# Reordering the head of a squared-ReLU MLP: x loads first, tail columns transposed in pairs, small loads moved between queues

## The chip, the cores and the metric

The kernel runs on one core of a Trainium2 chip. The metric is the device time of one execution in microseconds (us); lower is better. A profiled execution also gives a span, from the first to the last instruction, which is a little shorter than the device time.

## The reference

```python
# x (1, 2048, 576), w1 (576, 4608), b1 (4608), w2 (4608, 576), b2 (576), all bf16
h = jnp.einsum("bsd,df->bsf", x, w1) + b1
r = jnp.where(h > 0, h, 0)
h = r * r
out = jnp.einsum("bsf,fd->bsd", h, w2) + b2
```

It is a two-layer MLP whose hidden activation is the squared ReLU. The inner sizes are awkward in one place: D = 576 is four and a half times 128, so each contraction over D has four full chunks of 128 rows and a tail of 64.

## The kernel before, in words

The 2048 rows of x are worked in four blocks of 512 columns (`sb` 0 to 3). Phase A computes the hidden tile: for each of 36 groups of 128 hidden features it multiplies a piece of w1 with the transposed x block `xT` and writes `r = relu(h + b1)` on ACT (L176) and `hT = r * r` on DVE (L177). Phase B multiplies `hT` with w2 into the first 448 output columns (`phase_b`, L289), phase T does the last 128 output columns transposed (`phase_t`, L270, with the bias `b2T` added on ACT at L273).

Of the 36 feature groups, G = 4 are computed in `a_full` from full 128-row weights `w1n` plus the 64 tail rows `w1n8`; the other 32 are computed in `a_rows` as two halves of the array, 64 rows each, with weights `w_h` (`w1_h` in the code). For that the transposed block is kept in a nine-slot window buffer `xTw` with slots named E3 = 0, O = 1 to 4, SPC = 5, E = 6 to 8; slots 5 to 8 are copies, with upper and lower half partitions exchanged, that `dup_windows` writes on DVE (L119, L120).

Blocks 1 to 3 get their `xT` by DMA transposes on the SP queue (L126, L127). Block 0 can't wait for those. Its four row tiles of x are loaded plainly into `x_sb` (L72), transposed on PE against the identity matrix (`x_transpose`, L149), and copied out of PSUM by DVE and ACT (`x_copies`, L156 to L159). In the k_outer order, block 0's `a_full` weaves these transposes between groups of four matmuls of 256 columns (`part(h, k)`, L227), so that the first parts can run before all of x has been transposed. The tail chunk is taken as the 128 columns 448 to 575, a fifth transpose per row tile. After the parts come the four tail matmuls (`pair`, L203 and L205) and then `a_rows(0)`.

`keep` puts an instruction at its place in program order on its engine. Each engine then works its own list from top to bottom, and DMAs are issued from the lists of SP, ACT and POOL. Ahead of all this stand seven matmuls on constants (`WARM`, L63). POOL builds the identity, clears `b1_rows`, issues the load of b1 (L98) and of the last 128 values of b2 (`b2_col`, called b_col in the profile, L100), and then casts the latter into `b2T` (L102). All other loads are on SP, but for two x tiles on ACT. The SP list is: x 0, w1n 0, w1n 1, x 3, w1n 2, w1n 3, two `w_h` pieces, the two `w1n8` halves, twelve `w_h` pieces, the transposes of block 1, four `w_h` pieces, the broadcast of b2 (`b_bc`), four chunks of w2 (`w_sb`), the transposes of block 2.

Of the kernel before, what the change touches and what calls it, by code (L numbers as in the profile page):

```python
# [11 lines left out]
BF16 = mybir.dt.bfloat16  # L12
FP32 = mybir.dt.float32
# [4 lines left out]
def kernel(  # L18
# [9 lines left out]
    nc = tc.nc  # L28
    keep = tc.keep_in_program_order
    P = 128  # L30
    H = 64
    x2 = x.flatten_outer_dims()
    out2 = out.flatten_outer_dims()
    S, D = x2.shape
    F = w1.shape[1]
    NFT = F // P
    NC = D // H
    NK = NC // 2
    G = 4
    GW = G * P  # L40
# [4 lines left out]
    RT = SB // P  # L45
    DT = P
    DM = D - DT

    const = ctx.enter_context(tc.tile_pool(name="const", bufs=1))
    wpool = ctx.enter_context(tc.tile_pool(name="wpool", bufs=1))  # L50
# [5 lines left out]
    ps_h = ctx.enter_context(tc.tile_pool(name="ps_h", bufs=4, space=PSUM))  # L56
    ps_o = ctx.enter_context(tc.tile_pool(name="ps_o", bufs=4, space=PSUM))

    wps = ps_o.tile([P, 512], FP32, name="wps", tag="po")
    ones = nc.const_aps.tensor(1.0, [P, 512], BF16)  # L60
    WARM = [512] * 6 + [128]
    for i, n in enumerate(WARM):
        keep(nc.tensor.matmul(wps[:, 0:n], lhsT=ones[:, 0:P], rhs=ones[:, 0:n], start=True, stop=True))  # L63

    xs = const.tile([P, RT, D], BF16, name="x_sb")
    w1n = wpool.tile([P, NK, GW], BF16, name="w1n")
    w1n8 = wpool.tile([P, G // 2, P], BF16, name="w1n8")
    w1_h = wpool.tile([P, NC, FH], BF16, name="w1_h")
    w1_v = w1.rearrange("(c p) f -> p c f", p=H)

    def load_x(eng, rt):
        keep(eng.dma_start(out=xs[:, rt, :], in_=x2[rt * P:(rt + 1) * P, :]))  # L72

    def load_w1n(eng, k):
        keep(eng.dma_start(out=w1n[:, k, :], in_=w1[k * P:(k + 1) * P, 0:GW]))

    def load_w1n8(eng, h):
        src = w1[NK * P:D, 0:GW].rearrange("p (i h f) -> p i h f", h=2, f=P)
        keep(eng.dma_start(out=w1n8[h * H:(h + 1) * H, :, :], in_=src[:, :, h, :]))

    def load_w1(eng, h, j0, j1):
        keep(eng.dma_start(out=w1_h[h * H:(h + 1) * H, :, j0 * P:j1 * P],
                      in_=w1_v[:, :, GW + h * FH + j0 * P:GW + h * FH + j1 * P]))

    load_x(nc.sync, 0)
    load_x(nc.scalar, 1)
    load_w1n(nc.sync, 0)
    load_x(nc.scalar, 2)
    load_w1n(nc.sync, 1)
    load_x(nc.sync, 3)  # L90
    for k in range(2, NK):
        load_w1n(nc.sync, k)

    ident = const.tile([P, P], BF16, name="ident")
    make_identity(nc, ident[:])
    b1_rows = const.tile([P, P], BF16, name="b1_rows")
    nc.gpsimd.memset(b1_rows[:], 0.0)
    nc.gpsimd.dma_start(out=b1_rows[0:NFT, :], in_=b1.rearrange("(ft p) -> ft p", p=P))  # L98
    b2_col = const.tile([P, 1], BF16, name="b2_col")
    nc.gpsimd.dma_start(out=b2_col[:], in_=b2[DM:D].rearrange("(d o) -> d o", o=1))  # L100
    b2T = const.tile([P, 1], FP32, name="b2T")
    nc.gpsimd.tensor_copy(out=b2T[:], in_=b2_col[:])  # L102
    warm = const.tile([P, 1], FP32, name="warm")
    keep(nc.scalar.activation(out=warm[:], in_=nc.const_aps.tensor(0.0, [P, 1], FP32), func=ACT.Relu))

    E3, O, SPC, E = 0, 1, 5, 6
    LO_W = [O, O + 1, O + 2, O + 3, E, E + 1, E + 2, E3, SPC]
# [9 lines left out]
    def dup_windows(sb):  # L117
        xT = xT_blk[sb]
        keep(nc.vector.tensor_copy(out=xT[0:H, SPC:SPC + 4, :], in_=xT[H:P, E3:E3 + 4, :]))  # L119
        keep(nc.vector.tensor_copy(out=xT[H:P, SPC:SPC + 4, :], in_=xT[0:H, O:O + 4, :]))  # L120
# [7 lines left out]

    w2_sb = wpool.tile([P, NFT, D], BF16, name="w2_sb")
    w2_view = w2.rearrange("(ft p) d -> p ft d", p=P)  # L130
    W2CH = 9

    def load_w2(c):
        keep(nc.sync.dma_start(out=w2_sb[:, c * W2CH:(c + 1) * W2CH, :], in_=w2_view[:, c * W2CH:(c + 1) * W2CH, :]))
# [3 lines left out]
    alloc_xT(0)  # L138
    xT0 = xT_blk[0]
    HS = SB // 2  # L140
    tb_po = [ps_o.tile([P, 2, HS], BF16, name="tb", tag="po") for _ in range(2)]
    tb_ph = [ps_h.tile([P, 2, HS], BF16, name="tb", tag="ph") for _ in range(4)]
    half_banks = [tb_ph, None]

    def x_transpose(j, k):
        h, q = divmod(j, 2)
        qc = slice(q * P, (q + 1) * P)
        bank, slot, c0 = (half_banks[h][k], 0, k * P) if k < NK else (half_banks[h][2], 1, D - P)
        keep(nc.tensor.transpose(bank[:, slot, qc], xs[:, j, c0:c0 + P], ident[:]))  # L149

    def x_copies(h):
        hc = slice(h * HS, (h + 1) * HS)
        for k in range(NK):
            src = half_banks[h][k][:, 0, :]
            if k % 2 == 0:
                keep(nc.vector.tensor_copy(out=xT0[:, O + k, hc], in_=src))  # L156
            else:
                keep(nc.scalar.copy(out=xT0[:, O + k, hc], in_=src))
        keep(nc.vector.tensor_copy(out=xT0[:, E3, hc], in_=half_banks[h][2][:, 1, :]))  # L159


    b1T = const.tile([P, NFT], FP32, name="b1T")

    def make_b1T():
        b1T_ps = ps_o.tile([P, P], BF16, name="b1T_ps", tag="po")
        keep(nc.tensor.transpose(b1T_ps[:], b1_rows[:], ident[:]))  # L166
        keep(nc.vector.tensor_copy(out=b1T[:], in_=b1T_ps[:, 0:NFT]))

# [26 lines left out]
    def a_full(sb, order):  # L195
        xT = xT_blk[sb]
        banks = []
        for g in range(G):
            pool, tag = (ps_o, "po") if g < 2 else (ps_h, "ph")
            banks.append(pool.tile([P, SB], FP32, name="pn", tag=tag))  # L200

        def pair(i, start, stop):
            keep(nc.tensor.matmul(banks[2 * i][:], lhsT=w1n8[0:H, i, :], rhs=xT[0:H, SPC, :],  # L203
                             start=start, stop=stop, skip_group_check=order == "k_outer"))
            keep(nc.tensor.matmul(banks[2 * i + 1][:], lhsT=w1n8[H:P, i, :], rhs=xT[H:P, E3, :],  # L205
                             start=start, stop=stop, skip_group_check=order == "k_outer"))

        def full(g, k, start, stop):
            keep(nc.tensor.matmul(banks[g][:], lhsT=w1n[:, k, g * P:(g + 1) * P], rhs=xT[:, O + k, :],  # L209
                             start=start, stop=stop))  # L210

        if order == "rows_first":
            for i in (1, 0):
                pair(i, True, False)
            for g in (2, 3, 0, 1):
                for k in range(NK):
                    full(g, k, False, k == NK - 1)
                evac_h(sb, banks[g], g)
        else:
            if order == "k_outer":  # L220
                tb_new = [ps_h.tile([P, 2, HS], BF16, name="tb", tag="ph") for _ in range(2)]
                half_banks[1] = tb_new + tb_po

                def part(h, k):
                    hc = slice(h * HS, (h + 1) * HS)
                    for g in range(G):
                        keep(nc.tensor.matmul(banks[g][:, hc], lhsT=w1n[:, k, g * P:(g + 1) * P],  # L227
                                              rhs=xT[:, O + k, hc], start=(h == 0 and k == 0), stop=False,
                                              skip_group_check=True))

                for j in range(2):
                    for k in range(NK):
                        x_transpose(j, k)
                for j in range(2):
                    x_transpose(j, NK)
                x_copies(0)
                part(0, 0)
                for k in range(NK + 1):
                    x_transpose(2, k)
                part(0, 1)  # L240
                part(0, 2)
                for k in range(NK + 1):
                    x_transpose(3, k)
                x_copies(1)
                dup_windows(0)
                part(0, 3)
                part(1, 0)
                make_b1T()
                for k in range(1, NK):
                    part(1, k)  # L250
            else:
                for g in (2, 3, 0, 1):
                    for k in range(NK):
                        full(g, k, k == 0, False)
            for i in (1, 0):
                pair(i, False, True)
                evac_h(sb, banks[2 * i], 2 * i)
                evac_h(sb, banks[2 * i + 1], 2 * i + 1)
# [35 lines left out]
    for (j0, j1) in [(0, 1), (1, 2), (2, 4), (4, 6), (6, 8), (8, 10), (10, 12)]:  # L294
        load_w1(nc.sync, 0, j0, j1)
        load_w1(nc.sync, 1, j0, j1)
        if j0 == 0:
            load_w1n8(nc.sync, 0)
            load_w1n8(nc.sync, 1)
    load_xT(1)  # L300
    for (j0, j1) in [(12, 14), (14, 16)]:
        load_w1(nc.sync, 0, j0, j1)
        load_w1(nc.sync, 1, j0, j1)
    keep(nc.sync.dma_start(out=b2_bc[:], in_=b2.partition_broadcast(P)))
    for c in (0, 2, 1, 3):
        load_w2(c)
    load_xT(2)

# [51 lines left out]
```

## Time and profile before

| what | value |
|---|---|
| time, median of 3 runs | 290.72 us (290.65 to 291.53) |
| the profiled execution's own time | 291.46 us |
| its span | 289.6 us |
| granted TensorE clock | 1.000 |
| PE busy | 285.5 us, 99% of the span |
| ACT busy | 96.7 us, 33% |
| DVE busy | 78.6 us, 27% |
| POOL busy | 2.3 us, 1% |

The profiled execution took 1.86 us more than its span. PE is busy nearly all the time; its busy figure is an upper bound on useful work, since matmuls overlap and their ends are modelled. The other engines wait for PE. The columns of a timeline row are the start in us, the length in us, the engine, the line, the operation, its output and input, the number of instructions merged into the row, and in brackets the idle time before it with what ended it. In engine names, SPq and POOLq are the queues from which DMAs are issued; the length of such a row is the time of the issue, not of the transfer.

### The profile page before, as it was taken

Reading aid. Unit: us, or ns where it says so; the run is one execution under the profiler, and the core shown is the slowest. Engines: PE = TensorE matmul, PEld = TensorE weight load, DVE = VectorE, ACT = ScalarE, POOL = GpSimd, SP = SyncE. Lnnn points to the kernel's source line nnn. Section 1 sums busy time; section 2 is a strip of 40 time slices with the busy share of each in tenths; the row PEclk is TensorE's granted clock in tenths of the full one; section 3 lists DMA queues with packets and bytes.
Section 4 is the critical chain, followed back from the end, with each engine's and each line's share of the span. In section 5 each row is a group of like instructions: output and inputs, shape, how many; then the busy total and the mean of one; then the engine's idle time right before and its main releaser. Section 6 shows DMA issues by size and latency. Waiting matters only on the chain.

```text
span 289.6 us, 4693 instructions
## 1 busy us (share of the span) xinstructions
PE 285.5 (99%) x2027; PEld 139.9 (48%) x2032; DVE 78.6 (27%) x176; ACT 96.7 (33%) x154; POOL 2.3 (1%) x10
## 2 busy tenths in 40 slices
PE   8999999999999999999999999999999999999996
PEld 5544444444444555555544444444444455555555
DVE  1644554444500200000015444444440001100001
ACT  2566666666500000000027666666670000000000
POOL 3000000000000000000000000000000000000000
PEclk9999999999999999999999999999999999999999
DMA  7999999400001200000000000000000110000000
GB/s 198 221 245 188 308 389 212 92 0 2 0 14 25 52 16 18 16 16 18 16 16 2 1 2 0 2 0 2 0 2 0 36 38 16 16 16 19 33 16 18
DMA packets 31605, 16.52 MB, mean 57 GB/s; under 512 B 15700, under 2 KB 31584, under 8 KB 31584
## 3 DMA queue, kind: packets, MB, share of 16 engines
q1 hardware_dynamic: 31232, 15.91, 22.3%
q10 hardware_dynamic: 288, 0.30, 0.4%
q8 instruction: 16, 0.26, 0.4%
q14 instruction: 5, 0.04, 0.0%
q0 software_dynamic: 64, 0.01, 0.0%
HBM read 11.36 MB, written 2.36 MB: 47 GB/s over the span
## 4 chain that ended last, share of the span: by engine, by line
PE 98%; DMA 1%; issue 0%; DVE 0%
PE ph L188 42%; PE po L289 38%; PE pt L270 11%; PE pn L209 4%; PE pn L227 1%; DMA x_sb<-in_x_dram 1%; PE tb L149 1%; PE ph L190 1%; PE pn L203 1%; DVE o_sb L291 0%; PE b1T_ps L166 0%; PE pn L205 0%
## 5 line engine op out<-in xcount | busy, mean ns | idle before, releaser
L190 PE MATMUL ph<-xTw,w_h 64*128 64x512 bf16 x576 | 124.6, 376 | 0.0
L188 PE MATMUL ph<-xTw,w_h 64*128 64x512 bf16 x576 | 124.6, 376 | 0.0
L289 PE MATMUL po<-w_sb,hT 128*128 128x448 bf16 (+2 forms) x612 | 109.4, 341 | 0.0
L176 ACT ACTIVATE r<-ph,b1T 128x512 bf16<-128x512 f32 x128 | 81.1, 685 | 41.6 <-PE ph L190 41.6
L188 PEld LDWEIGHTS <-w_h 64*128 64x128 bf16 x576 | 54.1, 94 | 68.3
L289 PEld LDWEIGHTS <-hT 128*128 128x128 bf16 x612 | 58.5, 98 | 51.0
L177 DVE TENSOR_TENSOR hT<-r 128x512 bf16<-128x512 bf16 x144 | 61.2, 426 | 75.9 <-ACT r L176 75.5
L190 PEld LDWEIGHTS <-w_h 64*128 64x128 bf16 x576 | 54.1, 94 | 0.0
L291 DVE TENSOR_TENSOR o_sb<-po,b_bc 128x448 bf16<-128x448 f32 (+2 forms) x17 | 10.2, 597 | 125.8 <-PE po L289 125.8
L270 PE MATMUL pt<-hT,w_sb 128*128 128x512 bf16 x142 | 31.3, 379 | 0.1
L176 ACT ACTIVATE r<-pn,b1T 128x512 bf16<-128x512 f32 x16 | 10.3, 688 | 61.0 <-PE pn L205 59.6
L270 PEld LDWEIGHTS <-w_sb 128*128 128x128 bf16 x144 | 14.1, 98 | 17.0
L273 ACT ACTIVATE oT<-pt,b2T 128x512 bf16<-128x512 f32 x4 | 2.8, 688 | 28.3 <-PE pt L270 28.3
L209 PE MATMUL pn<-xTw,w1n 128*128 128x512 bf16 x45 | 10.4, 379 | 0.4 <-issue 0.3
L209 PEld LDWEIGHTS <-w1n 128*128 128x128 bf16 x48 | 4.5, 98 | 6.0 <-issue 0.8
L227 PE MATMUL pn<-xTw,w1n 128*128 128x256 bf16 x32 | 4.6, 295 | 0.0
L63 PE MATMUL wps<-const-bfloat16-1.0 128*128 128x512 bf16 (+1 forms) x7 | 2.8, 582 | 0.8 <-PEq L344 0.8
L227 PEld LDWEIGHTS <-w1n 128*128 128x128 bf16 x32 | 3.3, 107 | 0.5
L156 DVE COPY xTw<-tb 128x256 bf16<-128x256 bf16 x4 | 1.1, 292 | 6.7 <-PE tb L149 6.7
L119 DVE COPY xTw<-xTw 64x2048 bf16<-64x2048 bf16 x4 | 2.8, 690 | 0.2
L120 DVE COPY xTw<-xTw 64x2048 bf16<-64x2048 bf16 x4 | 2.7, 687 | 0.1
L149 PE MATMUL tb<-ident,x_sb 128*128 128x128 bf16 x20 | 2.4, 288 | 0.2 <-DMA x_sb<-in_x_dram 0.2
(23 smaller groups left out, 15.2 us busy)
## 6 DMA issues: line engine op xcount, KB each, us to landing
w_sb<-in_w_dram SPq DMA_DIRECT2D x4, 1296.0 KB, 12.7
w_h<-in_w_dram SPq DMA_DIRECT2D x14, 288.0 KB, 6.2
out_dram<-o_sb SPq DMA_DIRECT2D x15, 112.0 KB, 1.7
w_h<-in_w_dram SPq DMA_DIRECT2D x4, 144.0 KB, 3.5
w1n<-in_w_dram SPq DMA_DIRECT2D x4, 128.0 KB, 3.9
out_dram<-ot SPq DMA_DIRECT2D x4, 128.0 KB, 2.0
x_sb<-in_x_dram ACTq DMA_DIRECT2D x2, 144.0 KB, 2.9
x_sb<-in_x_dram SPq DMA_DIRECT2D x2, 144.0 KB, 3.4
```

What stands on the lines that cost most here:

```text
L63: keep(nc.tensor.matmul(wps[:, 0:n], lhsT=ones[:, 0:P], rhs=ones[:, 0:n], start=True, stop=True))
L149: keep(nc.tensor.transpose(bank[:, slot, qc], xs[:, j, c0:c0 + P], ident[:]))
L176: keep(nc.scalar.activation(out=r[:], in_=bank[:], func=ACT.Relu, bias=b1T[:, ft:ft + 1], scale=1.0))
L177: keep(nc.vector.tensor_tensor(out=hTs[sb][:, ft, :], in0=r[:], in1=r[:], op=ALU.mult))
L188: keep(nc.tensor.matmul(bx[:], lhsT=w1_h[0:H, LO_C[i], jc], rhs=xT[0:H, LO_W[i], :], start=(i == 0), stop=(i == NC - 1)))
L190: keep(nc.tensor.matmul(by[:], lhsT=w1_h[H:P, UP_C[i], jc], rhs=xT[H:P, UP_W[i], :], start=(i == 0), stop=(i == NC - 1)))
L203: keep(nc.tensor.matmul(banks[2 * i][:], lhsT=w1n8[0:H, i, :], rhs=xT[0:H, SPC, :], start=start, stop=stop, skip_group_check=order == "k_o ...
L209: keep(nc.tensor.matmul(banks[g][:], lhsT=w1n[:, k, g * P:(g + 1) * P], rhs=xT[:, O + k, :], start=start, stop=stop))
L227: keep(nc.tensor.matmul(banks[g][:, hc], lhsT=w1n[:, k, g * P:(g + 1) * P], rhs=xT[:, O + k, hc], start=(h == 0 and k == 0), stop=False, s ...
L270: keep(nc.tensor.matmul(pt[:], lhsT=w2_sb[:, ft, DM:D], rhs=hT[:, ft, :], start=(i == 0), stop=(i == NFT - 1)))
L289: keep(nc.tensor.matmul(po[:, 0:d1 - d0], lhsT=hT[:, ft, jj * P:(jj + 1) * P], rhs=w2_sb[:, ft, d0:d1], start=(i == 0), stop=(i == NFT - 1)))
L291: keep(nc.vector.tensor_tensor(out=o_sb[:, d0:d1], in0=po[:, 0:d1 - d0], in1=b2_bc[:, d0:d1], op=ALU.add))
```

## The change

The order of the first loads is now x 0 and x 2 on SP, x 1 and x 3 on ACT, then w1n 0 and 2 on SP and w1n 1 and 3 on ACT. The two `w1n8` loads move from SP to ACT and take the whole 512 columns for each half (1 KB a row, where they were two pieces of 256 bytes), and the load of b1 moves from POOL to ACT. `b1_rows` is cleared on DVE. The load of `b2_col` moves from POOL to SP, where it stands behind all `w_h` pieces; its cast into `b2T` stays on POOL. w2 comes in two chunks instead of four.

The transposes of block 0 are all done ahead of the parts. Each row tile has four transposes of full chunks. For the tail, POOL copies the 64 tail columns of two row tiles side by side into a new tile `xs8`, and one transpose then serves two row tiles: 16 + 2 transposes instead of 20. The new `x_copies_tail` takes them apart on DVE, with copies that also make the windows of block 0.

The PSUM banks are dealt differently (transposes and b1 in `ps_h`, the four `a_full` banks of block 0 in `ps_o`), and the seventh warm-up matmul has 256 columns instead of 128.

In the list that the built program gives each engine, POOL has after the identity these three instructions, in this order: the cast of `b2T`, which waits for the `b2_col` load, and the two copies into `xs8`. PE has the 16 full transposes, then the two tail transposes, each of which waits for its POOL copy, and then the first part. On SP, the load of `b2_col` stands behind two x tiles, two w1n chunks, fourteen `w_h` pieces, the two transposes of block 1 and four more `w_h` pieces.

```diff
-    wps = ps_o.tile([P, 512], FP32, name="wps", tag="po")
+    wps = ps_h.tile([P, 512], FP32, name="wps", tag="ph")
-    WARM = [512] * 6 + [128]
+    WARM = [512] * 6 + [256]
...
-    w1n8 = wpool.tile([P, G // 2, P], BF16, name="w1n8")
+    w1n8 = wpool.tile([P, GW], BF16, name="w1n8")
...
     def load_w1n8(eng, h):
-        src = w1[NK * P:D, 0:GW].rearrange("p (i h f) -> p i h f", h=2, f=P)
-        keep(eng.dma_start(out=w1n8[h * H:(h + 1) * H, :, :], in_=src[:, :, h, :]))
+        keep(eng.dma_start(out=w1n8[h * H:(h + 1) * H, :], in_=w1[NK * P:D, 0:GW]))
...
+    b1_rows = const.tile([P, P], BF16, name="b1_rows")
+    nc.vector.memset(b1_rows[:], 0.0)
     load_x(nc.sync, 0)
     load_x(nc.scalar, 1)
-    load_w1n(nc.sync, 0)
-    load_x(nc.scalar, 2)
-    load_w1n(nc.sync, 1)
-    load_x(nc.sync, 3)
-    for k in range(2, NK):
-        load_w1n(nc.sync, k)
+    load_x(nc.sync, 2)
+    load_x(nc.scalar, 3)
+    for k in range(NK):
+        load_w1n(nc.sync if k % 2 == 0 else nc.scalar, k, k + 1)
...
-    b1_rows = const.tile([P, P], BF16, name="b1_rows")
-    nc.gpsimd.memset(b1_rows[:], 0.0)
-    nc.gpsimd.dma_start(out=b1_rows[0:NFT, :], in_=b1.rearrange("(ft p) -> ft p", p=P))
-    b2_col = const.tile([P, 1], BF16, name="b2_col")
-    nc.gpsimd.dma_start(out=b2_col[:], in_=b2[DM:D].rearrange("(d o) -> d o", o=1))
-    b2T = const.tile([P, 1], FP32, name="b2T")
-    nc.gpsimd.tensor_copy(out=b2T[:], in_=b2_col[:])
     warm = const.tile([P, 1], FP32, name="warm")
     keep(nc.scalar.activation(out=warm[:], in_=nc.const_aps.tensor(0.0, [P, 1], FP32), func=ACT.Relu))
+    for h in range(2):
+        load_w1n8(nc.scalar, h)
+    keep(nc.scalar.dma_start(out=b1_rows[0:NFT, :], in_=b1.rearrange("(ft p) -> ft p", p=P)))
...
-    W2CH = 9
+    W2CH = 18
...
-    def x_transpose(j, k):
+    def x_transpose(j):
         h, q = divmod(j, 2)
-        qc = slice(q * P, (q + 1) * P)
-        bank, slot, c0 = (half_banks[h][k], 0, k * P) if k < NK else (half_banks[h][2], 1, D - P)
-        keep(nc.tensor.transpose(bank[:, slot, qc], xs[:, j, c0:c0 + P], ident[:]))
+        for k in range(NK):
+            bank, slot = PLACE[k]
+            keep(nc.tensor.transpose(tb[h][bank][:, slot, q * P:(q + 1) * P], xs[:, j, k * P:(k + 1) * P], ident[:]))
+
+    def x_transpose_tail(h):
+        keep(nc.gpsimd.tensor_copy(out=xs8[:, 2 * h:2 * h + 2, :], in_=xs[:, 2 * h:2 * h + 2, NK * P:D]))
+        keep(nc.tensor.transpose(tb[1][0][:, 2, h * P:(h + 1) * P], xs8[:, 2 * h:2 * h + 2, :], ident[:]))
+
+    def x_copies_tail():
+        src = tb[1][0][:, 2, :].rearrange("p (h t) -> p h t", h=2)
+        for q in range(2):
+            keep(nc.vector.tensor_copy(out=xT0_q[H:P, E3, :, q, :], in_=src[q * H:(q + 1) * H, :, :]))
+        for q in range(2):
+            keep(nc.vector.tensor_copy(out=xT0_q[0:H, SPC, :, q, :], in_=src[q * H:(q + 1) * H, :, :]))
+        keep(nc.vector.tensor_copy(out=xT0[0:H, E:E + 3, :], in_=xT0[H:P, O:O + 3, :]))
+        keep(nc.vector.tensor_copy(out=xT0[0:H, E3, :], in_=xT0[H:P, O + 3, :]))
+        keep(nc.vector.tensor_copy(out=xT0[H:P, SPC:SPC + 4, :], in_=xT0[0:H, O:O + 4, :]))
 
     def x_copies(h):
         hc = slice(h * HS, (h + 1) * HS)
-        for k in range(NK):
-            src = half_banks[h][k][:, 0, :]
-            if k % 2 == 0:
-                keep(nc.vector.tensor_copy(out=xT0[:, O + k, hc], in_=src))
-            else:
-                keep(nc.scalar.copy(out=xT0[:, O + k, hc], in_=src))
-        keep(nc.vector.tensor_copy(out=xT0[:, E3, hc], in_=half_banks[h][2][:, 1, :]))
+        for k in (0, 1):
+            keep(nc.vector.tensor_copy(out=xT0[:, O + k, hc], in_=tb[h][0][:, k, :]))
+        keep(nc.scalar.copy(out=xT0[:, O + 2:O + 4, hc], in_=tb[h][1][:, 0:2, :]))
...
                 for j in range(2):
-                    for k in range(NK):
-                        x_transpose(j, k)
-                for j in range(2):
-                    x_transpose(j, NK)
+                    x_transpose(j)
                 x_copies(0)
-                part(0, 0)
-                for k in range(NK + 1):
-                    x_transpose(2, k)
-                part(0, 1)
-                part(0, 2)
-                for k in range(NK + 1):
-                    x_transpose(3, k)
+                for j in range(2, RT):
+                    x_transpose(j)
                 x_copies(1)
-                dup_windows(0)
-                part(0, 3)
+                for h in range(2):
+                    x_transpose_tail(h)
+                x_copies_tail()
+                for k in range(NK):
+                    part(0, k)
                 part(1, 0)
                 make_b1T()
...
-        if j0 == 0:
-            load_w1n8(nc.sync, 0)
-            load_w1n8(nc.sync, 1)
     load_xT(1)
     for (j0, j1) in [(12, 14), (14, 16)]:
         load_w1(nc.sync, 0, j0, j1)
         load_w1(nc.sync, 1, j0, j1)
+    b2_col = const.tile([P, 1], BF16, name="b2_col")
+    keep(nc.sync.dma_start(out=b2_col[:], in_=b2[DM:D].rearrange("(d o) -> d o", o=1)))
+    b2T = const.tile([P, 1], FP32, name="b2T")
+    nc.gpsimd.tensor_copy(out=b2T[:], in_=b2_col[:])
     keep(nc.sync.dma_start(out=b2_bc[:], in_=b2.partition_broadcast(P)))
-    for c in (0, 2, 1, 3):
+    for c in range(2):
         load_w2(c)
```

More of the change, by code (lines that the diff above doesn't have):

```diff
@@ L72, in load_x, with load_w1n @@
         keep(eng.dma_start(out=xs[:, rt, :], in_=x2[rt * P:(rt + 1) * P, :]))
-    def load_w1n(eng, k):
-        keep(eng.dma_start(out=w1n[:, k, :], in_=w1[k * P:(k + 1) * P, 0:GW]))
+    def load_w1n(eng, k0, k1):
+        src = w1[k0 * P:k1 * P, 0:GW].rearrange("(k p) f -> p k f", p=P)
+        keep(eng.dma_start(out=w1n[:, k0:k1, :], in_=src))
     def load_w1n8(eng, h):
-        src = w1[NK * P:D, 0:GW].rearrange("p (i h f) -> p i h f", h=2, f=P)
-        keep(eng.dma_start(out=w1n8[h * H:(h + 1) * H, :, :], in_=src[:, :, h, :]))
+        keep(eng.dma_start(out=w1n8[h * H:(h + 1) * H, :], in_=w1[NK * P:D, 0:GW]))
     def load_w1(eng, h, j0, j1):
@@ L140 @@
     HS = SB // 2
-    tb_po = [ps_o.tile([P, 2, HS], BF16, name="tb", tag="po") for _ in range(2)]
-    tb_ph = [ps_h.tile([P, 2, HS], BF16, name="tb", tag="ph") for _ in range(4)]
-    half_banks = [tb_ph, None]
-    def x_transpose(j, k):
-        h, q = divmod(j, 2)
-        qc = slice(q * P, (q + 1) * P)
-        bank, slot, c0 = (half_banks[h][k], 0, k * P) if k < NK else (half_banks[h][2], 1, D - P)
-        keep(nc.tensor.transpose(bank[:, slot, qc], xs[:, j, c0:c0 + P], ident[:]))
+    tb = [[ps_h.tile([P, 4, HS], BF16, name="tb", tag="ph") for _ in range(2)] for _ in range(2)]
@@ new lines @@
+    PLACE = [(0, 0), (0, 1), (1, 0), (1, 1)]
+    xs8 = const.tile([P, RT, H], BF16, name="xs8")
+    xT0_q = xT0.rearrange("p c (h q t) -> p c h q t", h=2, q=2)
+    def x_transpose(j):
+        h, q = divmod(j, 2)
+        for k in range(NK):
[4 more added lines that the diff above has]
+        keep(nc.tensor.transpose(tb[1][0][:, 2, h * P:(h + 1) * P], xs8[:, 2 * h:2 * h + 2, :], ident[:]))
@@ L162 @@
+        keep(nc.scalar.copy(out=xT0[:, O + 2:O + 4, hc], in_=tb[h][1][:, 0:2, :]))
     b1T = const.tile([P, NFT], FP32, name="b1T")
     def make_b1T():
-        b1T_ps = ps_o.tile([P, P], BF16, name="b1T_ps", tag="po")
+        b1T_ps = ps_h.tile([P, P], BF16, name="b1T_ps", tag="ph")
         keep(nc.tensor.transpose(b1T_ps[:], b1_rows[:], ident[:]))
@@ L198, in a_full @@
         for g in range(G):
-            pool, tag = (ps_o, "po") if g < 2 else (ps_h, "ph")
+            pool, tag = (ps_o, "po") if g < 2 or order == "k_outer" else (ps_h, "ph")
             banks.append(pool.tile([P, SB], FP32, name="pn", tag=tag))
         def pair(i, start, stop):
-            keep(nc.tensor.matmul(banks[2 * i][:], lhsT=w1n8[0:H, i, :], rhs=xT[0:H, SPC, :],
+            keep(nc.tensor.matmul(banks[2 * i][:], lhsT=w1n8[0:H, 2 * i * P:(2 * i + 1) * P], rhs=xT[0:H, SPC, :],
                              start=start, stop=stop, skip_group_check=order == "k_outer"))
-            keep(nc.tensor.matmul(banks[2 * i + 1][:], lhsT=w1n8[H:P, i, :], rhs=xT[H:P, E3, :],
+            keep(nc.tensor.matmul(banks[2 * i + 1][:], lhsT=w1n8[H:P, (2 * i + 1) * P:(2 * i + 2) * P], rhs=xT[H:P, E3, :],
                              start=start, stop=stop, skip_group_check=order == "k_outer"))
@@ L220, in a_full @@
             if order == "k_outer":
-                tb_new = [ps_h.tile([P, 2, HS], BF16, name="tb", tag="ph") for _ in range(2)]
-                half_banks[1] = tb_new + tb_po
                 def part(h, k):
```

## The prediction

> **What bounds the kernel now.** I read the page's totals first, then the chain of waits in order of time for the head, then the timelines of POOL and SP, since the change moves work on those two.
>
> ```profile
> span 289.6 us, 4693 instructions
> PE 285.5 (99%) x2027; PEld 139.9 (48%) x2032; DVE 78.6 (27%) x176; ACT 96.7 (33%) x154; POOL 2.3 (1%) x10
> ```
>
> PE has no slack: whatever holds PE for a microsecond adds a microsecond. The change touches only the head, so the head is what I price. Its chain of waits (start, length, what):
>
> ```profile
> 0.73 2.99 DMA x_sb<-in_x_dram
> 3.73 0.04 issue
> 3.77 1.25 PE tb L149 x10
> 5.02 0.86 PE pn L227 x4
> 5.88 0.53 PE tb L149 x5
> 6.42 0.98 PE pn L227 x8
> 7.40 0.28 PE tb L149 x5
> 7.68 0.87 PE pn L227 x8
> 8.55 0.06 PE b1T_ps L166
> 8.61 1.31 PE pn L227 x12
> 9.92 0.32 PE pn L203
> ```
>
> From 3.77 us the chain stays on PE until the tail matmuls (L203; the timeline starts them at 9.85). There is no hole left to fill. The first four parts take 0.86/4 = 0.215 us each and eight later ones 0.87/8 = 0.109 us: PE runs at half rate until a little after 6 us, although PE has been at work since 0.78.
>
> Now POOL and SP, from the timelines of these engines (start, length, engine; brackets: idle before):
>
> ```profile
> 2.14 0.56 POOL L100 DMA_DIRECT2D b_col<-in_b_dram  x1
> 5.72 0.18 POOL L102 CAST b2T<-b_col 128x1 f32<-128x1 bf16 x1 [3.03 <-DMA b_col<-in_b_dram]
> ```
>
> ```profile
> 18.29 4.57 SPq L126 DMA_TRANSPOSE xTw<-in_x_dram  x1
> 22.91 1.25 SPq L127 DMA_TRANSPOSE xTw<-in_x_dram  x1
> 24.21 2.65 SPq L82 DMA_DIRECT2D w_h<-in_w_dram  x4
> 26.91 0.82 SPq L304 DMA_DIRECT2D b_bc<-in_b_dram  x1
> 27.77 10.21 SPq L134 DMA_DIRECT2D w_sb<-in_w_dram  x4
> ```
>
> The load of b_col is issued at 2.14, and its cast on POOL waits 3.03 us for it. Nothing stands behind that cast on POOL, so the wait is free. On SP, the slot just behind the last `w_h` piece, where the change puts this load, comes at 26.9 us. The DMA issues say when things from there land: for the window of the last `w_h` issue (26.2 us), and on the page,
>
> ```profile
> w_h<-in_w_dram SPq DMA_DIRECT2D x1, 288.0 KB, 6.6
> ```
>
> ```profile
> b_bc<-in_b_dram SPq DMA_DIRECT2D x1, 144.0 KB, 6.5
> ```
>
> so the last `w_h` lands at 26.2 + 6.6 = 32.8 and b_bc at 26.9 + 6.5 = 33.4 us.
>
> **What the Trainium skill says.** "Trainium Architecture — The Big Picture", section "Inside one NeuronCore": each engine has its own instruction stream and the engines meet only through semaphores. So what stands behind a waiting instruction on its engine waits too. The trace agrees for SP: its L275 waits 77.6 us for ACT, and SP issues nothing meanwhile. For POOL no case is shown. "DMA: Bandwidth & Descriptors", section "Queues, rings and completion order": descriptors of a ring are consumed in order, and the completion increment lands only after every earlier write from that DMA engine. The trace agrees: the issue-to-landing time of the 288 KB pieces grows from about 4 us (at 7 us) to 7.7 us (at 12 us) as the backlog grows, and b_bc lands 0.6 us after the piece ahead of it. "TensorE: Matmul & The Clock Gate", section "What's actually happening": an idle window of about 3.4 us puts PE back to half rate, and a busy one of about 3.4 us, with a free-running phase, restores it. The half-rate parts above agree with the start; no stall of that length is in the trace of before.
>
> **The change, part by part.**
>
> *The wait.* POOL's list is now: identity, cast of b2T, two copies into xs8. PE's list is: 16 transposes, two tail transposes on xs8, then all 32 parts. The cast waits for b2_col, the xs8 copies stand behind the cast, the tail transposes wait for the copies, and every part stands behind the tail transposes. So PE stops after 16 transposes, about 5.8 us, until b2_col lands. On PE, everything is behind it; ACT and DVE wait for PE.
>
> *When b2_col lands.* SP loses ahead of it two w1n issues (0.9 us) and two w1n8 issues (1.29), and has the same number of x tiles. But the early part of SP's list is paced by landings: DMA shares are near full from 3 us on, and the bytes ahead are the same but for w1n8, now 2 x 64 KB instead of 2 x 32 KB in half as many pieces. So I move the issue only from 26.9 to 26.4, and the last `w_h` landing from 32.8 to 32.3. b2_col, 0.2 KB, follows it by half of b_bc's 0.6: **32.6 us**. Bounds: 29.4, if small loads overtake the backlog (26.9 + 2.5, what a 32 KB w1n8 piece took); 38.4, if it lands only with the first w2 chunk behind it (27.8 + 10.6).
>
> *From there to the first part.* 0.08 us from landing to cast (before: 5.64 to 5.72), cast 0.18. A POOL copy of 128 x 128 is not in the trace; the nearest POOL rows, of 128 x 128 elements, are a memset (0.21) and the affine select (0.29). I take 0.3 each, bounds 0.2 and 0.5. After the second, some 0.2 for the semaphore, weight load and transpose: 32.6 + 0.26 + 0.6 + 0.2 = 33.7 us (33.5 to 34.1).
>
> *Parts to tail matmuls.* PE has then been idle for 27 us. By the skill's window the half rate lasts 3.4 to 6.8 us more; I take 5. Then 22 parts at 0.215 (4.7), 10 at 0.109 (1.1) and the b1 transpose (0.1) make 5.9; bounds 5.3 and 7.0. The tail matmuls start at 33.7 + 5.9 = 39.6 instead of 9.85: **+29.8 us**.
>
> *What costs nothing.* Two transposes fewer (2 x 0.11 at half rate) and 128 more warm-up columns (0.1) lie ahead of the stall. So do the order of x and w1n, and the moved w1n8 and b1 loads and the b1_rows clear (DVE 0.2, ACT's three issues of about 0.5): all have 27 us to land in. ACT's two 128x512 copies instead of four of 0.38, and DVE's four plain ones (0.29 each), also end in the stall. The tail copies on DVE start with the tail transposes: four of 64x256 at about 0.29 and three window copies of 1536, 512 and 2048 columns at 0.69 per 2048 (0.5 + 0.2 + 0.7), 2.6 us. They are needed after 5.3 or more; without that cover they would cost their whole 2.6. On SP, b2_col delays b_bc and w2 by one issue (about 0.5). In before the last w2 chunk lands at 34.7 + 13.3 = 48.0; it is needed at 76.6, after the change at 106. Two w2 chunks for four is as well covered, and the transposes of blocks 1 to 3 come with the same or more room. The new banks add no wait: in the stall all are emptied. What followed the tail matmuls was PE-bound and stays so.
>
> *Sum.* 291.46 + 29.8 = 321.2 us against the profiled execution, whose span would be 319.4. That execution stands 0.74 above the median of the runs shown, so against the median 290.72 + 29.8 = **320.5 us**.
>
> **Rivals.**
>
> *The load overtakes the backlog* and lands at 29.4: 3.2 us less, 317.3. For it: it is a tiny transfer. Against: its pieces lie in the same rings behind 1.1 MB of `w_h`, and b_bc didn't overtake.
>
> *The load lands late*, with the w2 chunk at 38.4: 5.8 more, 326.3. For it: 128 pieces of 2 bytes, which no load on SP in before has. Against: b_bc also lay ahead of w2 and landed at 33.4.
>
> *No stall, and not slower.* The place is POOL's cast: were the xs8 copies to go ahead of it, or b2_col to land before the 16 transposes end, PE would go on. The point from which it decides is a landing at about 5.3 us (5.8 less 0.26 for the cast and 0.3 for a copy); beyond it each microsecond costs one. Then the head has two transposes less (0.2) and perhaps the 0.17 idle before x 0: at most 0.4 us gained, 290.3. Against: SP can't reach the load before some 20 others, and the instruction lists leave no other order.
>
> *The change doesn't do what it says*: 18 transposes and the new load order are in the lists; they just don't bear on the end.
>
> **How the numbers follow.** A measurement of this kernel can tell about 0.3%, 0.9 us, from no change. The stall with a landing behind the backlog: 0.82, and 317.5 to 323.5 by the bounds of copies, rate and issue time (1 us either way). Overtaking: 0.06. Late: 0.05. No stall: 0.07, of which 0.04 within 0.3% and 0.03 faster, if the loads help more than I see. The predicted time is that of the likeliest, 320.5. The range 315.5 to 324 takes in the overtaking case and leaves out the late one and the no-stall one.
>
> **What would show it.** Right: on POOL a wait of some 27 us in front of the b2T cast, released by the b_col DMA; on PE one idle stretch from about 6 to 33 us ahead of the tail transposes; parts at 0.215 us after it; tail matmuls at about 39.6; the same PE spacing after. Wrong: xs8 copies before 10 us; or b_col landing well before the last `w_h`; or PE idle in some other place.

## The result and the profile after

The changed kernel takes 319.31 us (median of 6 runs, 318.36 to 320.25) against 291.00 us (6 runs, 290.65 to 291.53): a ratio of 1.0969, with a 95% interval of 1.0944 to 1.0994. Its profiled execution took 318.36 us, with a span of 316.3 us. The ratios in the experiments below are each to runs of the kernel before that were taken beside them (medians 290.94 to 291.10 us).

The page's totals and two of its rows in slices (40 slices of 7.9 us; digits are tenths, of busy time or of the full clock):

```profile
span 316.3 us, 4698 instructions
PE 286.5 (91%) x2030; PEld 139.7 (44%) x2030; DVE 79.3 (25%) x180; ACT 96.4 (30%) x152; POOL 1.4 (0%) x9
...
PE   5000999999999999999999999999999999999996
...
PEclk9555899999999999999999999999999999999999
```

PE is busy for 286.5 us, one more than before; the span is 26.7 longer. Nearly all of it is one hole, in the second to fourth slices, with the granted clock at half in the hole and for some microseconds after it. POOL's timeline says what closes the hole (start, length, engine, line; in brackets the idle time before and what ended it):

```profile
1.01 0.29 POOL masks.py:199 TENSOR_SCALAR_AFFINE_SELECT ident<-ident 128x128 bf16<-128x128 bf16 x1
30.91 0.19 POOL L302 CAST b2T<-b_col 128x1 f32<-128x1 bf16 x1 [29.61 <-DMA b_col<-in_b_dram]
31.03 0.53 POOL L149 COPY xs<-x_sb 128x128 bf16<-128x128 bf16 x2
```

The two copies into xs8 (called xs in the profile) need nothing but x, which has long landed. They start behind a cast of 128 numbers that waits 29.6 us for its load. PE's timeline is the other side of it:

```profile
4.50 0.81 PE L146 MATMUL tb<-ident,x_sb 128*128 128x128 bf16 x8 [0.30 <-DMA x_sb<-in_x_dram]
31.38 0.53 PE L150 MATMUL tb<-ident,xs 128*128 128x128 bf16 x2 [26.07 <-POOL xs L149]
31.70 3.67 PE L230 MATMUL pn<-xTw,w1n 128*128 128x256 bf16 x20
35.20 0.22 PE L172 MATMUL b1T_ps<-ident,b_rows 128*128 128x128 bf16 x1
35.26 1.47 PE L230 MATMUL pn<-xTw,w1n 128*128 128x256 bf16 x12
36.66 0.39 PE L209 MATMUL pn<-xTw,w1n 64*128 64x512 bf16 x1
```

PE stops for 26.07 us ahead of the tail transposes, and the tail matmuls (L209) start at 36.66 us. In the timeline of before they start at 9.85:

```profile
9.85 0.39 PE L203 MATMUL pn<-xTw,w1n 64*128 64x512 bf16 x1
```

From there to the end of the span it is 316.3 - 36.66 = 279.64 us in the changed kernel; before it was 289.6 - 9.85 = 279.75: everything behind the head is as it was. SP's timeline shows where the load went:

```profile
16.76 4.93 SPq L122 DMA_TRANSPOSE xTw<-in_x_dram  x1
21.74 1.25 SPq L123 DMA_TRANSPOSE xTw<-in_x_dram  x1
23.03 2.65 SPq L82 DMA_DIRECT2D w_h<-in_w_dram  x4
25.73 0.87 SPq L300 DMA_DIRECT2D b_col<-in_b_dram  x1
```

It is issued at 25.73 and takes 5.1 us to land, at 30.8. One thing in this profile misleads: the page's chain of waits puts the stretch ahead of the copies down to a DMA of b_bc and to SP's issues, not to b_col. The list of waits and POOL's timeline name the load that held the cast, and the first two experiments below confirm it.

### The profile page after: what moved, and what is told of

Same layout as the page of the kernel before. It is cut to its first block, busy times and chain, and to the rows that moved or that the text cites. A ratio compares the mean times of both kernels' runs of the same rounds, so it can differ in the third digit from the quotient of the medians.

```text
span 316.3 us, 4698 instructions
## 1 busy us (share of the span) xinstructions
PE 286.5 (91%) x2030; PEld 139.7 (44%) x2030; DVE 79.3 (25%) x180; ACT 96.4 (30%) x152; POOL 1.4 (0%) x9
## 4 chain that ended last, share of the span: by engine, by line
PE 89%; SPq 6%; DMA 3%; ACTq 0%; issue 0%; POOL 0%; DVE 0%
PE ph L194 39%; PE po L287 34%; PE pt L268 10%; SPq L82 4%; PE pn L215 3%; SPq L122 2%; PE pn L230 2%; DMA b_bc<-in_b_dram 1%; DMA w1n<-in_w_dram 1%; PE ph L196 1%; PE pn L209 1%; SPq L123 0%; SPq L300 0%; ACTq L72 0%; PE tb L150 0%
## 5 line engine op out<-in xcount | busy, mean ns | idle before, releaser
L268 PE MATMUL pt<-hT,w_sb 128*128 128x512 bf16 x144 | 31.4, 379 | 0.0
L150 PEld LDWEIGHTS <-xs 128*128 128x128 bf16 x2 | 0.2, 104 | 26.4 <-POOL xs L149 26.2
L271 ACT ACTIVATE oT<-pt,b2T 128x512 bf16<-128x512 f32 x4 | 2.7, 687 | 28.3 <-PE pt L268 28.3
L209 PE MATMUL pn<-xTw,w1n 64*128 64x512 bf16 x8 | 2.4, 379 | 0.0
```

What stands on the lines that cost most here:

```text
L209: keep(nc.tensor.matmul(banks[2 * i][:], lhsT=w1n8[0:H, 2 * i * P:(2 * i + 1) * P], rhs=xT[0:H, SPC, :], start=start, stop=stop, skip_grou ...
L268: keep(nc.tensor.matmul(pt[:], lhsT=w2_sb[:, ft, DM:D], rhs=hT[:, ft, :], start=(i == 0), stop=(i == NFT - 1)))
```

## Experiments

The theory: the whole loss is POOL's order, a cast with a late load ahead of two copies that PE needs, plus a smaller part for the half clock after the stall. The rivals: the late load costs in itself, through SP or the DMA rings; or the new order of loads and transposes holds PE.

### The cast behind the copies

```diff
-    nc.gpsimd.tensor_copy(out=b2T[:], in_=b2_col[:])
...
     a_full(0, "k_outer")
+    keep(nc.gpsimd.tensor_copy(out=b2T[:], in_=b2_col[:]))
```

> The changed kernel, with one instruction moved: the cast of b2T stands on POOL behind the two xs8 copies instead of ahead of them. The load of b2_col keeps its place on SP. Theory (POOL's order is the whole loss): the cast still waits until about 31 us, but nothing stands behind it; PE's idle stretch of 26 us goes, the tail matmuls start at 10.0 us (16 transposes to 5.3, tail transposes to 5.7, parts held to 7.3 by ACT's copies of x, which the changed trace has at 6.7 to 7.8) and the time is 290.5 to 292.5 us, about that of before. Rival (the late b2_col, the new load order or the transposes all ahead of the parts hold PE by themselves): more than 300 us, with PE idle at another wait.

Measured: 291.93 us (291.82 to 292.58), ratio to before 1.0033 (1.0021 to 1.0045). POOL's timeline:

```profile
3.71 0.29 POOL L149 COPY xs<-x_sb 128x128 bf16<-128x128 bf16 x1 [2.42 <-DMA x_sb<-in_x_dram]
4.44 0.29 POOL L149 COPY xs<-x_sb 128x128 bf16<-128x128 bf16 x1 [0.43 <-DMA x_sb<-in_x_dram]
32.75 0.19 POOL L309 CAST b2T<-b_col 128x1 f32<-128x1 bf16 x1 [28.02 <-DMA b_col<-in_b_dram]
```

The cast waits as long as ever, 28 us, and costs nothing. Moving one instruction takes back 319.31 - 291.93 = 27.4 of the 28.3 us. A third of a per cent remains; PE's timeline shows it as short waits in the head (the row of the tail matmuls is the last):

```profile
5.35 0.27 PE L150 MATMUL tb<-ident,xs 128*128 128x128 bf16 x2 [0.47 <-DVE xTw L165]
5.70 0.61 PE L230 MATMUL pn<-xTw,w1n 128*128 128x256 bf16 x4
6.54 0.61 PE L230 MATMUL pn<-xTw,w1n 128*128 128x256 bf16 x4 [0.23 <-DMA w1n<-in_w_dram]
7.81 1.47 PE L230 MATMUL pn<-xTw,w1n 128*128 128x256 bf16 x12 [0.66 <-ACT xTw L166]
9.51 0.23 PE L172 MATMUL b1T_ps<-ident,b_rows 128*128 128x128 bf16 x1 [0.22 <-DMA b_rows<-in_b_dram]
...
10.98 0.39 PE L209 MATMUL pn<-xTw,w1n 64*128 64x512 bf16 x1
```

The time fell in the range named, but the tail matmuls came at 10.98, 1 us later than expected: the wait for ACT's copies ended at 7.8 us instead of 7.3, and the other three waits were not expected. 10.98 - 9.85 = 1.13 us is just what this profiled execution (292.58 us) took more than that of before (291.46). So the new order of loads and transposes, the other rival, costs about 1 us and not 28.

### The load early, the cast ahead of the copies

```diff
-    keep(nc.sync.dma_start(out=b2_col[:], in_=b2[DM:D].rearrange("(d o) -> d o", o=1)))
...
     make_identity(nc, ident[:])
+    b2_col = const.tile([P, 1], BF16, name="b2_col")
+    nc.gpsimd.dma_start(out=b2_col[:], in_=b2[DM:D].rearrange("(d o) -> d o", o=1))
```

> The changed kernel, with the load of b2_col issued early on POOL's own queue; the cast stays ahead of the xs8 copies. Theory: the load lands at about 4.5 us (issue at 1.0, 3.5 to landing as before), the cast is over at 4.8, the copies at 5.4, and the time is that of the kernel with the cast last, 290.5 to 292.5 us. Rival (POOL's copies are slow or wait for something else): the stall stays, over 300 us.

Measured: 292.20 us (291.67 to 292.26), ratio 1.0032 (1.0019 to 1.0046), with the cast at 5.23 us and the copies done at 5.9. Here the order on POOL is that of the change and the load alone is moved; the stall is gone as well. So it takes both, the late load and the order, to make the 28 us.

### The late load in the kernel before

```diff
-    nc.gpsimd.dma_start(out=b2_col[:], in_=b2[DM:D].rearrange("(d o) -> d o", o=1))
-    nc.gpsimd.tensor_copy(out=b2T[:], in_=b2_col[:])
...
+    keep(nc.sync.dma_start(out=b2_col[:], in_=b2[DM:D].rearrange("(d o) -> d o", o=1)))
+    nc.gpsimd.tensor_copy(out=b2T[:], in_=b2_col[:])
     keep(nc.sync.dma_start(out=b2_bc[:], in_=b2.partition_broadcast(P)))
```

> The kernel before, with only the load of b2_col moved to SP behind all w_h pieces, as the change has it. POOL has nothing behind the cast here. Theory: POOL waits about 26 us for the load, and the time stays at 290.7 to 291.5 us: the wait costs only through what stands behind it. Rival (a late b2_col costs in itself, through SP's list or the DMA rings): 1 us or more slower.

Measured: 291.20 us (14 runs, 290.79 to 293.29), ratio 1.0008 (0.9995 to 1.0020), no difference. Its list of waits (engine, tile and line, what was waited for, us in total, times, longest):

```profile
POOL b2T L303 <- DMA b_col<-in_b_dram: 31.0, 1, 31.0
```

This is a longer wait than the 29.6 us in the changed kernel, where moving the cast took back 27.4 us, and it is free. The rival that the late load costs in itself falls.

### The load midway

```diff
     for (j0, j1) in [(0, 1), (1, 2), (2, 4), (4, 6), (6, 8), (8, 10), (10, 12)]:
         load_w1(nc.sync, 0, j0, j1)
         load_w1(nc.sync, 1, j0, j1)
+        if j0 == 4:
+            b2_col = const.tile([P, 1], BF16, name="b2_col")
+            keep(nc.sync.dma_start(out=b2_col[:], in_=b2[DM:D].rearrange("(d o) -> d o", o=1)))
+            b2T = const.tile([P, 1], FP32, name="b2T")
+            nc.gpsimd.tensor_copy(out=b2T[:], in_=b2_col[:])
```

> The changed kernel, with the load of b2_col behind eight w_h pieces on SP instead of eighteen and the block-1 transposes; POOL's order is that of the change. Theory (each microsecond of landing is one of time): issue at about 9.5 us, landing at about 14.8 (5.3 behind the backlog), 16 us before that of the changed kernel, so 318.4 - 16 = 302.4 us (300 to 304). Rival (the load overtakes the backlog of w_h): landing at 12 or before and 299 us or less. Rival (POOL is held by something else): 318 us.

Measured: 304.35 us (303.13 to 305.05), ratio 1.0442 (1.0420 to 1.0464), a little above the range named. From SP's timeline:

```profile
10.78 1.07 SPq L297 DMA_DIRECT2D b_col<-in_b_dram  x1
```

and from POOL's:

```profile
16.50 0.19 POOL L299 CAST b2T<-b_col 128x1 f32<-128x1 bf16 x1 [15.20 <-DMA b_col<-in_b_dram]
```

The issue came at 10.78, not 9.5, and the landing 5.7 us later, at 16.5. The landing is 14.4 us before the changed kernel's, and the profiled execution (305.05 us) is 13.3 us under the other's. The 1.1 us between is the half clock: in this run's chain all 20 parts ahead of the b1 transpose take 4.27 us, in the changed kernel's 3.46 (0.8 us), and the next eight still take 0.15 us each on average instead of 0.109 (0.3 us). So the time follows the landing one to one, apart from how long the half clock lasts after it. Nor does the load overtake the backlog: 5.7 us for 256 bytes.

### The stall filled with matmuls

```diff
+                for _ in range(FILL):
+                    keep(nc.tensor.matmul(banks[0][:], lhsT=ones[:, 0:P], rhs=ones[:], start=True, stop=True,
+                                          skip_group_check=True))
                 for h in range(2):
                     x_transpose_tail(h)
```

With FILL = 110:

> The changed kernel, with 110 matmuls of 512 columns on constants (results overwritten) between the 16 full transposes and the two tail transposes, so that PE is at work for most of the stall; they take about 24 us and should end by 29.7, ahead of the landing. Theory (the half rate after the stall is a second, smaller cost): the 32 parts and the b1 transpose take 3.6 us instead of 4.8, and the time is 1.2 us less than the changed kernel's at an equal landing, some 318 us against 319.3. Rival (the idle time has no price beyond its length): the parts take 4.8 us as in the changed kernel. The run also says whether a busy PE changes when b_col lands: 30.8 us in the changed kernel's profile with PE idle, 32.7 in the kernel with the cast last and PE busy.

Measured: 320.50 us (319.95 to 320.80), ratio 1.1013 (1.0999 to 1.1027), not less than the changed kernel but more. The filler ended at 30.05, the load landed later than hoped, at 32.2, and PE was idle for 2.7 us until the tail transposes started at 32.74. That was enough to bring the half clock. From the windows of PE (stretch in us, its length, PE busy and the number of instructions, granted clock, DMA share, GB/s):

```profile
30.00:31.00 1.00, 0.06 (x1) 1.00 1.33 228
31.00:32.00 1.00, 0.00 (x0) 1.00 1.08 185
32.00:33.00 1.00, 0.25 (x2) 1.00 0.91 297
33.00:34.00 1.00, 1.00 (x8) 0.71 1.06 357
34.00:35.00 1.00, 1.00 (x6) 0.50 1.08 389
35.00:36.00 1.00, 1.00 (x7) 0.50 1.09 393
36.00:37.00 1.00, 1.00 (x8) 0.58 1.09 393
```

The clock goes to half when PE is already back at work: a window at half for its last 0.58 us has the mean of 0.71, one at half for its first 0.84 us that of 0.58, so the half clock lasts from 33.4 to 36.8 us. From the first part to the tail matmuls it took 38.36 - 33.05 = 5.3 us. So this run does not part the theory from its rival. A longer filler, with FILL = 122, does:

> The changed kernel with 122 filler matmuls on constants in the stall instead of 110. With 110, PE was idle for 2.7 us after the filler, and the half rate came back all the same (from 33.3 to 36.8 us), so the parts and the b1 transpose took 5.3 us. Now the filler should end at about 32.7, when the tail transposes may start (landing at 32.2 as with 110). Theory (the half rate comes from the idle window): no half rate, parts and b1 transpose in 3.6 us, tail matmuls at 36.6 instead of 38.4, the time 1.7 us under that with 110 fillers, 318.8 us. Rival (the half rate comes from the parts themselves): 5.3 us and 320.5 again.

Measured: 318.08 us (317.75 to 318.88), ratio 1.0930 (1.0910 to 1.0950). The same windows in this run:

```profile
31.00:32.00 1.00, 0.69 (x4) 1.00 0.98 171
32.00:33.00 1.00, 0.24 (x2) 1.00 0.99 324
33.00:34.00 1.00, 1.00 (x10) 1.00 1.08 392
34.00:35.00 1.00, 1.00 (x11) 1.00 1.08 391
```

The load landed at 32.2 as with the shorter filler. With 1.1 us idle the full clock stays, and the parts and the b1 transpose take 36.70 - 33.05 = 3.65 us. The rival, that the half rate comes from the parts themselves, falls. The longer filler is 2.4 us faster than the shorter one, of which 1.65 is this difference. The recorded mean clocks of the runs say the same: 0.999 or 1.000 in all five with the longer filler; with the shorter one 0.995 in the two faster runs (319.95 and 320.26 us) and 0.988 and 0.989 in the two slower ones, which had about twice as long at half rate. In the changed kernel the same stretch takes 4.96 us, so the half clock cost its profiled execution 1.3 us of the 26.8.

### The scatter of the landing

The changed kernel was run again, first once and then four times.

> The changed kernel once more, for the scatter of its landing. The six runs span 318.4 to 320.3 us, and the profile was of the fastest. Theory: b_col lands between 30.8 and 32.7 us, and the time follows it one to one (318.4 to 320.3).

> The changed kernel once more, timed, for the scatter and the landing with PE idle. Two profiles had b_col land at 30.8 and 30.9 us with PE idle; four with PE busy at 32.2 to 33.1. Theory (a busy PE slows the DMA stream): landing at 31 again, and most runs at 318.3 to 319.5, under those with 110 fillers (320.0 to 320.8). Rival (scatter of the landing, whatever PE does): a landing of 31.5 or later, and runs spread over 318.3 to 320.8.

Measured: 318.35 us with b_col landing at 30.9 us, and 318.76 us (318.39 to 319.35), ratio 1.0952 (1.0932 to 1.0972), with b_col landing at 31.3 in a profile of 319.35 us. Three landings with PE idle lie at 30.8, 30.9 and 31.3; those of both fillers at 32.2, of the kernel with the cast last at 32.7. Two fillers and three idle runs don't overlap, which favours a slower DMA stream under a busy PE: from 16 to 26 us it moved 213 to 218 GB/s with PE idle, 200 and 195 with the fillers. What in PE's work slows it was not tried. With the 110 filler the delay lies ahead of the load (SP issues it at 27.09 us instead of 25.7 to 26.3), and from issue to landing it takes 5.1 us as with PE idle.

The landing alone does not make the scatter: in the 319.35 us profile it is 0.5 us later than in the 318.36 us one, and the half clock costs 0.6 us more (the 20 parts take 4.28 us by the timeline instead of 3.67). The slowest of the eleven runs, at 320.25 us, has a mean clock of 0.952, nine others 0.957; twice the missing share of the span makes about 30.5 us at half rate instead of 27.2. One run, of 319.52 us, was recorded with 0.999, so with almost no time at half rate. No profile of it was kept, and why it was not faster stays open.

### What remains with the stall gone

With the cast last, ACT's copies of x came at 7.2 us. On ACT they stand behind the issue of the b1 load, which the change put there, and that issue waits until 6.57 us. The next kernel is that with the cast last, with the b1 load back on POOL, ahead of the copies:

```diff
-    keep(nc.scalar.dma_start(out=b1_rows[0:NFT, :], in_=b1.rearrange("(ft p) -> ft p", p=P)))
...
     make_identity(nc, ident[:])
+    nc.gpsimd.dma_start(out=b1_rows[0:NFT, :], in_=b1.rearrange("(ft p) -> ft p", p=P))
```

> The kernel with the cast last on POOL, and the load of b1 moved from ACT back to POOL's queue, ahead of the xs8 copies. In the kernel with the cast last, ACT's copies of x stand behind the issue of the b1 load, which waits on ACT until 6.6 us for a w1n chunk to land[...]; PE is idle 0.66 us for those copies, 0.22 for b_rows, 0.23 for a w1n chunk and 0.47 for DVE's copies. Theory (ACT's list is the rest of the loss): ACT copies at 4.4 to 5.5, both first waits go, the tail matmuls start at 9.6 to 10.1 instead of 11.0, and the time is 290.5 to 291.1, 0.9 to 1.4 us below the kernel with the cast last. Rival (the landing of w1n holds the parts anyway): the tail matmuls stay at 10.8 or later and the time at 291.9.

Measured: 291.72 us (290.89 to 291.97), ratio 1.0024 (1.0014 to 1.0034). The waits went as expected; from PE's timeline:

```profile
5.83 0.27 PE L150 MATMUL tb<-ident,xs 128*128 128x128 bf16 x2 [0.37 <-DVE xTw L165]
6.04 2.36 PE L230 MATMUL pn<-xTw,w1n 128*128 128x256 bf16 x20
8.24 0.22 PE L172 MATMUL b1T_ps<-ident,b_rows 128*128 128x128 bf16 x1
8.29 1.47 PE L230 MATMUL pn<-xTw,w1n 128*128 128x256 bf16 x12
9.70 0.39 PE L209 MATMUL pn<-xTw,w1n 64*128 64x512 bf16 x1
```

The tail matmuls start at 9.70, but the median missed the expected range by 0.6 us, and the intervals of this kernel and of the one with the cast last overlap. The profile is of a run at 291.30, one of the faster ones. In profiles of the kernel before and of its variant with the late load the same start lies at 9.85 and 8.70, so one profile of the head is good to about 1 us, and the last 0.2% can't be read from it. These two differ in how long PE is slow at the start: by their chains the first four parts take 0.215 us each in the one and 0.15 in the other, and the five transposes behind them 0.106 and 0.056. The clock row of the page does not show this; it has 9 from the first slice in both. What it does show is that the new head still has a hole of 0.37 us for DVE's copies that the woven order of before did not have.

The last kernel is this one with x and w1n loaded in the order of before:

```diff
-    load_x(nc.sync, 2)
-    load_x(nc.scalar, 3)
-    for k in range(NK):
-        load_w1n(nc.sync if k % 2 == 0 else nc.scalar, k, k + 1)
+    load_w1n(nc.sync, 0, 1)
+    load_x(nc.scalar, 2)
+    load_w1n(nc.sync, 1, 2)
+    load_x(nc.sync, 3)
+    for k in range(2, NK):
+        load_w1n(nc.sync, k, k + 1)
```

> As the kernel with b1 on POOL, but x and w1n loaded in the order and on the queues of before. Theory (loading x first helps once all transposes stand ahead of the parts): the fourth x tile lands about 1 us later, the transposes of it and POOL's second copy hold all parts, and the time is 0.5 to 1.5 us above that kernel. Rival (the order of loads makes no difference): within 0.3 us of it.

Measured: 293.38 us (291.74 to 295.22), ratio 1.0079 (1.0054 to 1.0104), 1.7 us above the kernel with b1 on POOL, a little more than expected. From its list of waits:

```profile
POOL xs L151 <- DMA x_sb<-in_x_dram: 3.5, 2, 2.0
...
PE tb L148 <- DMA x_sb<-in_x_dram: 1.1, 1, 1.1
```

So loading x first is worth something once all transposes stand ahead of the parts; it is a cure for the new order, and with both the head is no shorter than before. None of the versions beats the kernel before.

## Why the prediction was right, and its sizes

The forecast was 320.5 us, in a range of 315.5 to 324; it came out at 319.31.

- **The wait and its place** were as forecast: POOL's cast, released by the b_col DMA; the xs8 copies and PE's tail transposes behind it; one hole from 5.3 to 31.4 us (forecast: from 5.8). The cast-last, early-load and late-load-in-before runs show each link by itself.
- **The landing** was put at 32.6 and came at 30.8 to 31.3. The issue term, 26.4, was near (25.7 to 26.3), but the 6.2 us from there to the landing, taken from two loads of one profile of before, were too many: the load took 5.0 to 5.1. In the cast-last kernel it took 6.3 and landed at 32.7, 0.1 from the forecast. PE being idle or busy does not explain this term by itself: with PE at work the same step took 4.9 us (late load in before), 5.1 and 5.5 (fillers) and 6.0 to 6.3 (the three kernels with the cast last). What sets it stays open.
- **The load overtaking the backlog, or landing late with w2**: neither. In the changed kernel's profile the last `w_h` piece landed at about 30.7 us, b_col at 30.8 and b_bc at 32.
- **From landing to the first part**: 1.1 us forecast, 31.70 - 30.8 = 0.9 measured. A POOL copy of 128 x 128 takes 0.29 (0.3 taken), but the two come 0.53 after the first one's start, and PE takes 0.06 less than the 0.2 given after them.
- **Parts to tail matmuls**: 5.9 forecast, with 22 parts at half rate; 4.96 measured, with 12. A later profile, 0.6 us longer there at 0.106 us a part, had about 18. The low bound of 5.3 was too high for two reasons. The half clock was counted from the parts, and 0.3 us of it had passed with the tail transposes. And it lasted 3.0 us from the first tail transpose (31.4 to 34.4), less than the 3.4 us that the prediction's estimate had as its least; in the two later profiles it was 2.8 and 4.3 us. The filler shows that the term is real: without half clock it is 3.65.
- **The sum**: 26.81 instead of 29.8 us on the profiled execution, of which the landing makes 1.8, the parts 0.9 and the chain 0.2. That execution was among the fastest of its kernel and that of before among the slowest; between medians it is 28.3. So half of the 3.0 us by which the sum was too long does not appear in the comparison of the medians; that is the scatter of single executions, and no merit of the forecast.
- **What was costed at nothing** cost nothing behind the stall: DVE's tail copies end at 34.6 us, 2 us ahead of the tail matmuls, and the later part of the kernel is as long as before to 0.1 us. One entry was right only through the stall: the b1 load on ACT holds ACT's copies of x up to 6.7 us in the changed kernel. When the stall is taken away, this comes up as PE's longest wait in the head, 0.66 us.
- **The no-stall rival** put the time without the wait at 290.3 at best, a gain of up to 0.4. The kernels with the cast last, with the early load and with b1 on POOL lie 0.7 to 1.1 us above before instead: the rival left out the waits for ACT's and DVE's copies.

## What to carry to other kernels

An instruction that waits for a late load is free only as long as nothing urgent stands behind it on its engine; before work is put on an idle engine, read that engine's list for waits, and before a load is moved later, find its reader and what the reader's engine does next. A wait of 31 us cost nothing here, and one of 29.6 us cost 27 us, for the place of one instruction. After a stall count the slow clock too, and when a stall is removed look for the waits that it covered.

## What was not expected of the hardware

The clock fell to half after only 2.7 us without matmuls, and it did so after PE had resumed (the 110-filler run, 33.4 to 36.8 us); 1.1 us of idle time left it at full.

The half clock came in multiples of one length. In the three profiles of the changed kernel it lasted 27.3 us each time (7.1 to 34.4, 7.0 to 34.3 and 8.8 to 36.1), with the load midway 13.65 (8.78 to 22.43) and with the 110 filler 3.41 (33.43 to 36.84): 8, 8, 8, 4 and 1 times 3.41 (the ends are read from windows of 0.04 us). How these periods lay to the stall differed from run to run. The clock fell 1.8, 2.0, 3.4, 3.3 and 3.4 us after PE had stopped, and in the first four it came back 3.0, 2.8, 4.3 and 5.5 us after PE had resumed. So the price of the half clock behind a stall is not fixed by the length of the stall alone.

A load of 256 bytes behind a backlog of 288 KB pieces took 5.0 to 5.7 us to land with PE idle (5.7 with the load midway) and 4.9 to 6.3 with PE at work.
